# Attention and a two-layer feed-forward on one core: token and feature tiles padded by 32 and 64 bytes

## The chip, the cores and the metric

The kernel runs on one core of one Trainium2 chip. The metric is the time of one execution on the device in microseconds, lower is better; a measured time is the median of several executions.

## The reference, cut to what matters

Eight heads of attention over 8 sequences of 576 tokens with head size 64, then a feed-forward network over all 4608 tokens. Half of the heads see a local window of 32 positions, the other half every 32nd position.

```python
scores = scale * np.matmul(q, k.transpose(0, 1, 3, 2))
...
scores = np.where(masks[None, :, :, :], scores, -1000000000.0)
attn = exp(scores - max) / (sum + 1e-09)
attn_out = np.matmul(attn, v)
x = attn_out.transpose(0, 2, 1, 3).reshape(B * S, H * D)   # 4608 tokens x 512
h = np.maximum(x @ w_in, 0.0)                              # 512 -> 2048
return (h * h @ w_out).astype(np.float32)                  # 2048 -> 512
```

## The kernel before

The 4608 tokens are cut into 12 chunks of 384 (`TC`). For each chunk there are 16 groups of 128 hidden features. TensorE has two big jobs for each chunk and feature group.

`up` (through `products`, line 611) makes a tile of hidden features: 12 products of a 128x128 piece of `w_in` (the stationary operand, which is loaded into the array) with 384 tokens of x (the moving operand, which streams through it). Every number is held as a high and a low part, so x has four tiles for a chunk: `xlh`, `xll` from the local heads, `xsh`, `xsl` from the strided ones, each with two halves of 384 numbers for each of the 128 partitions. ScalarE then squares the rectified tile and writes its high part `gh`, VectorE its low part `gl`.

`down` (line 661) multiplies these: for each of three groups of 128 tokens, three products in which a 128x128 piece of `gh` or `gl` is stationary and 512 columns of `w_out` move.

From chunk 2 on the order is a cycle of four feature groups: four `up` (48 matmuls of line 611), four `down` (36 matmuls of line 661). Chunk 1 has the same in cycles of two. Ahead of each half of a cycle stands a visit of up to four small matmuls for the next chunks' attention: `s` (line 278, scores of a local head) and `o` (line 337, its output), as o, s, o, s. All other engines prepare x and the features beside this. Chunk 0 is written out by hand in the table `START`. The order on each engine is fixed by the program.

Where the tiles lie: pools are laid out one behind the other in each partition, first the weights (8192 bytes a tile), then `xpool` with two buffers of each of the four x tags, then `gpool` with three of `gh` and three of `gl`, then the rest. An x tile holds 2 x 384 numbers of four bytes, 3072 bytes, and a feature tile 384 numbers, 1536 bytes. All three sizes are multiples of 512, so each weight, x and feature tile starts at the same remainder modulo 512 bytes (it is 320 in the built program). The pieces taken from them also start at multiples of 512 bytes from the tile's start. So the moving and the stationary operand of every matmul of lines 611 and 661 are a multiple of 512 bytes apart. The distance is called zero in this text.

For the small matmuls it is not always so. The stationary `qx` piece of window w starts 384 w bytes into its tile and the moving `kx` piece 4 `at[w]` bytes into its own, and both tiles start at the same remainder. `windows` gives `at` = 0, 96, 192, 288 where both halves of a chunk lie behind each other in one sequence (chunks 6 to 11), and 0, 96, 224, 320 where they don't (chunks 0 to 5). So windows 2 and 3 of a local head have distance 0 in chunks 6 to 11 and distance 128 in chunks 2 to 5; they are visited between `up` and `down`.

```python
for n, (kt, w, s) in enumerate(parts):
    ...
    done = nc.tensor.matmul(h_ps[c, j][:, :TC], wi[p][w][:, wsl], x["ls"[kt // 2], s][:, kt % 2, :], ...)
...
    done = nc.tensor.matmul(into, g[:, t * P : (t + 1) * P], wo[p][w][:, wsl], ...)
```

Of the kernel before, what the change touches and what calls it, by code (L numbers as in the profile page):

```python
# [8 lines left out]
F32R = mybir.dt.float32r  # L9
# [13 lines left out]
P = 128  # L23
TC = 384
# [9 lines left out]
SCALE = 1.0 / 8.0  # L34
NEG = -8.0e9
JH = 8

NPLAIN = 2
NFIRST = 30
# [79 lines left out]
def attn_moe(ctx: ExitStack, tc, qk_l, v_l, qk_d, v_d, qk_p, v_p, f_s, q_s, k_s, v_s, w_in, w_out, masks, eye, out):  # L119
# [4 lines left out]
    xpool = pool("xpool", 2)  # L124
    gpool = pool("gpool", 3)
# [97 lines left out]
    def x_tiles(c):  # L223
        if c not in xt:
            xt[c] = {
                (kind, part): xpool.tile([P, 2, TC], F32R, name=f"x{kind}{part}{c}", tag=f"x{kind}{part}")
                for kind in "ls"
                for part in "hl"
            }
        return xt[c]  # L230
# [9 lines left out]
    class Head:  # L240
# [88 lines left out]
        def outputs(self, a, bank):  # L329
            par, hp = D * (self.h % 2), self.h // 2  # L330
            if a == 0 and not par:
                outs[self.c, hp] = self.buf(lpool, "st", TC, "st", bufs=1)
            o = psum(bank, f"o{a}{self.u}")

            def product(w):
                v, p = self.vx[:, w].rearrange("p t d -> p (t d)"), self.px[:, :, w * QC : (w + 1) * QC]
                return nc.tensor.matmul(o[:, 2 * QC * (w - a) : 2 * QC * (w - a + 1)], v, p, start=True, stop=True)  # L337

            def rest():
                x = x_tiles(self.c)  # L340
                st = outs[self.c, hp]
                ov = o[:, : 4 * QC].rearrange("p (w t q) -> p w t q", w=2, t=2)
                part = st[par : par + D, a * QC : (a + 2) * QC].rearrange("p (w q) -> p w q", w=2)
                nc.scalar.copy(part, ov[D:, :, 0, :])  # L344
                nc.vector.tensor_add(part, ov[:D, :, 1, :], part)
                nc.vector.tensor_add(part, ov[:D, :, 0, :], part)
                if par and a:
                    dst = [x["l", s][:, hp, :] for s in "hl"]
                    last["a"] = nc.scalar.copy(dst[0], st)
                    last["g"] = nc.gpsimd.tensor_sub(dst[1], st, f32(dst[0]))  # L350

            return [lambda w=w: product(w) for w in (a, a + 1)], rest
# [19 lines left out]
    class Pair:  # L372
# [80 lines left out]
        def out(self, a):  # L453
            x = x_tiles(self.at)
            if self.local:
                return self.s[a][:, :TC], [x["l", s][:, self.pr, :] for s in "hl"]
            r0 = D * self.pr
            by_i = lambda t: t[r0 : r0 + D].rearrange("p (s i r) -> p s i r", s=2, r=STR)
            return self.s[a][r0 : r0 + D, :TC].rearrange("p (s r i) -> p s i r", s=2, i=SI), [by_i(x["s", s][:, a, :]) for s in "hl"]
# [10 lines left out]
    class Range:  # L470


        def __init__(self, c, b, i0, i1, col):
            self.at, self.b, self.i0, self.i1, self.col = c, b, i0, i1, col
            self.ni, self.u = i1 - i0, f"{c}_{b}"
            self.short, self.prods = i1 == SI, {}
            self.scored = [(i, a, min(JH, i + 1 - a)) for i in range(i0, i1) for a in range(0, i + 1, JH)]
            self.mixed = []
            for i in range(i0, i1):
                step = -(-D // -(-(i + 1) // JH))  # L480
                self.mixed += [(i, a, min(step, D - a)) for a in range(0, D, step)]
# [24 lines left out]
        def m(self, n):  # L506
            i, a, m = self.scored[n]
            prod = spool.tile([P, JH * D], F32, name=f"pq{self.u}_{i}_{a}", tag="prod", bufs=2)
            pv = prod[:, : m * D].rearrange("p (j d) -> p j d", d=D)
# [28 lines left out]
        def p(self, n):  # L538
            i, a, nd = self.mixed[n]
            m, il = i + 1, i - self.i0  # L540
            prod = spool.tile([P, JH * D], F32, name=f"pp{self.u}_{i}_{a}", tag="prod", bufs=2)
            self.prods["p", n] = pv = prod[:, : m * nd].rearrange("p (d j) -> p d j", j=m)
# [11 lines left out]
        def out(self):  # L554
            x = x_tiles(self.at)
            cols = slice(self.col, self.col + self.ni * STR)
            return [x["s", s][:, :, cols] for s in "hl"], self.xf.rearrange("p a i r -> p a (i r)")
# [56 lines left out]
    def up(c, j):  # L614
        parts = [(kt, w, s) for kt in range(4) for w, s in ((0, "h"), (0, "l"), (1, "h"))]
        if j < 2:

            parts.sort(key=lambda i: i[0] < 2 and i[2] == "l")
        done = products(c, j, parts, True, True)
        g = h_ps.pop((c, j))[:, :TC]  # L620
        nc.scalar.activation(g, g, AF.Relu)  # L621
        nc.scalar.activation(g, g, AF.Square)  # L622
        feats[c, j] = feature_high(c, j, g), feature_low(c, j, g)
        return done

    def feature_high(c, j, g):
        gh = gpool.tile([P, TC], F32R, name=f"gh{c}_{j}", tag="gh")
        gl = gpool.tile([P, TC], F32R, name=f"gl{c}_{j}", tag="gl")
        g_tiles[c, j] = gh, gl
        return nc.scalar.copy(gh, g)  # L630

# [4 lines left out]
    def feature(j, what):  # L636

        g = h_ps[0, j][:, :TC]
        r = p_t[j % 2].rearrange("p w q -> p (w q)")
        if what == "R":  # L640
            nc.scalar.activation(r, g, AF.Relu)
        elif what == "G":
            nc.vector.scalar_tensor_tensor(out=g, in0=g, scalar=0.0, in1=r, op0=ALU.max, op1=ALU.mult)
        elif what == "K":
            last["a"] = feature_high(0, j, g)
        else:
            last["v"] = feature_low(0, j, g)
# [246 lines left out]
    for s in range(2 * NFT, NS, GROUP):  # L894
        c, j = divmod(s, NFT)
# [94 lines left out]
```

## Time and profile before

| what | value |
|---|---|
| median of 3 runs | 861.84 us (861.84 to 862.65) |
| span of the profiled execution, first to last instruction | 861.0 us |
| TensorE busy | 855.1 us of the span (99%) |
| VectorE, ScalarE, GpSimd busy | 643.0, 554.4, 662.8 us |
| granted TensorE clock | 1.00 over the span |

The profile gives the profiled execution's span; the median lies 0.84 us above it, which is taken as what lies around the first and the last instruction. Busy time of TensorE is the union of overlapping records, so it says that something was under way, not how fast. How fast is read from the starts of matmuls that follow each other.

### The profile page before, as it was taken

What the parts mean: (1) busy time and instruction counts of PE and PEld (TensorE: products, weight loads), DVE (VectorE), ACT (ScalarE), POOL (GpSimd) and SP (SyncE); (2) the same over time, 40 slices, a digit from 0 to 9 for tenths busy, and PEclk for the clock granted to TensorE, in tenths of its full rate; (3) what the DMA queues carried; (4) which work ended last, traced back from release to release, by engine and by line L of the source; (5) the groups of instructions that cost most, each with busy time, mean ns of one, the idle gap of its engine ahead of it and who ended that gap; (6) DMA issues with size and microseconds to landing.
All of it is one profiled execution on the core that took longest, in us unless ns stands there. A gap on an engine that the chain in (4) does not pass through costs nothing.

```text
span 861.0 us, 14577 instructions
## 1 busy us (share of the span) xinstructions
PE 855.1 (99%) x4748; PEld 781.5 (91%) x4748; DVE 643.0 (75%) x1893; ACT 554.4 (64%) x1473; POOL 662.8 (77%) x733
## 2 busy tenths in 40 slices
PE   9999999999999999999999999999999999999998
PEld 8988889999999999999999999999998999899987
DVE  7998788877787887797888788778878788852111
ACT  7997777676666765775577656665667567634423
POOL 5898788888788898898979989988987998850000
PEclk9999999999999999999999999999999999999999
DMA  9955522313122032113122111302211111000000
GB/s 356 364 218 158 171 81 83 108 37 108 56 88 81 27 133 76 32 63 113 31 69 71 58 54 56 99 27 81 78 54 63 45 60 38 1 2 37 1 1 37
DMA packets 27227, 71.32 MB, mean 83 GB/s; under 512 B 3024, under 2 KB 9680, under 8 KB 25616
## 3 DMA queue, kind: packets, MB, share of 16 engines
q1 hardware_dynamic: 26720, 70.00, 24.2%
q8 instruction: 37, 0.61, 0.3%
q10 hardware_dynamic: 432, 0.39, 0.1%
q14 instruction: 38, 0.31, 0.1%
HBM read 60.95 MB, written 9.44 MB: 82 GB/s over the span
## 4 chain that ended last, share of the span: by engine, by line
PE 95%; ACT 3%; DVE 1%; POOL 1%; issue 0%; POOLq 0%; ACTq 0%
PE h L611 45%; PE y L661 45%; PE s L278 2%; PE o L337 2%; ACT e L418 1%; ACT raw L184 1%; PE b L409 0%; PE w_ps L772 0%; ACT z L205 0%; POOL pq L510 0%; ACT pt L441 0%; DVE sc L515 0%; ACT xsh L463 0%; PE b L451 0%; DVE gl L634 0%
## 5 line engine op out<-in xcount | busy, mean ns | idle before, releaser
L661 PE MATMUL y<-w,gh 128*128 128x512 f32 x1152 | 364.8, 390 | 0.0
L661 PEld LDWEIGHTS y<-w,gh 128*128 128x128 f32 x1152 | 216.2, 188 | 43.8
L661 PE MATMUL y<-w,gl 128*128 128x512 f32 x576 | 224.3, 389 | 0.0
L611 PE MATMUL h<-xsh,w 128*128 128x384 f32 x768 | 223.2, 334 | 0.0
L611 PE MATMUL h<-xlh,w 128*128 128x384 f32 x768 | 216.9, 335 | 0.2 <-DVE gl L634 0.2
L510 POOL TENSOR_TENSOR pq<-ks,qs 128x512 f32<-128x512 f32 (+2 forms) x192 | 198.3, 1052 | 19.1 <-DVE sc L515 16.1
L543 POOL TENSOR_TENSOR pp<-vs,sc 128x448 f32<-128x448 f32 (+10 forms) x192 | 190.0, 1015 | 17.8 <-DVE qs L547 15.3
L634 DVE TENSOR_TENSOR gl<-h,gh 128x384 fp32r<-128x384 f32 x192 | 105.9, 552 | 79.2 <-ACT gh L630 76.9
L515 DVE TENSOR_REDUCE sc<-pq 128x8 f32<-128x512 f32 (+4 forms) x228 | 119.3, 534 | 33.9 <-POOL pq L510 30.6
L621 ACT ACTIVATE h<-h 128x384 f32<-128x384 f32 x176 | 83.8, 476 | 90.9 <-PE h L611 81.9
L611 PEld LDWEIGHTS h<-xlh,w 128*128 128x128 f32 x768 | 140.0, 188 | 1.8 <-DVE gl L634 0.6
L611 PEld LDWEIGHTS h<-xsh,w 128*128 128x128 f32 x768 | 141.2, 188 | 0.0
L661 PEld LDWEIGHTS y<-w,gl 128*128 128x128 f32 x576 | 108.2, 188 | 20.8
L611 PE MATMUL h<-xsl,w 128*128 128x384 f32 x384 | 125.7, 334 | 0.0
L611 PE MATMUL h<-xll,w 128*128 128x384 f32 x384 | 122.4, 335 | 0.0
L547 DVE TENSOR_REDUCE qs<-pp 128x64 f32<-128x448 f32 (+11 forms) x192 | 106.8, 563 | 20.4 <-POOL pp L543 17.9
L630 ACT CAST gh<-h 128x384 fp32r<-128x384 f32 x192 | 91.5, 478 | 14.0 <-PE y L661 7.5
L344 ACT COPY st<-o 64x192 f32<-64x192 f32 x80 | 25.1, 315 | 110.2 <-PE o L337 107.6
L311 DVE STREAM_TRANSPOSE p_t<-e 32x128 f32<-32x128 f32 x240 | 72.4, 301 | 21.9 <-ACT e L303 15.8
L622 ACT ACTIVATE h<-h 128x384 f32<-128x384 f32 x176 | 83.7, 475 | 4.7
L611 PEld LDWEIGHTS h<-xsl,w 128*128 128x128 f32 x384 | 71.9, 188 | 0.0
L611 PEld LDWEIGHTS h<-xll,w 128*128 128x128 f32 x384 | 71.6, 188 | 0.2
(111 smaller groups left out, 1122.2 us busy)
## 6 DMA issues: line engine op xcount, KB each, us to landing
qk<-qk_l SPq DMA_DIRECT2D x24, 400.0 KB, 3.1
y<-ysb SPq DMA_DIRECT2D x35, 256.0 KB, 2.1
raw<-w_in SPq DMA_DIRECT2D x7, 1024.0 KB, 10.3
qk<-qk_l SPq DMA_DIRECT2D x16, 416.0 KB, 3.3
vs<-v_s SPq DMA_DIRECT2D x10, 576.0 KB, 3.9
raw<-w_out SPq DMA_DIRECT2D x5, 1024.0 KB, 11.9
v<-v_l SPq DMA_DIRECT2D x40, 128.0 KB, 2.1
ks<-k_s SPq DMA_DIRECT2D x8, 576.0 KB, 3.8
```

Source lines behind the costliest of these rows:

```text
L311: nc.vector.transpose(out=pt[STR * k : STR * (k + 1), :, STR * r : STR * (r + 1)], in_=self.e.rearrange("p (w k) -> p w k", k=KW)[STR * r ...
L344: nc.scalar.copy(part, ov[D:, :, 0, :])
L510: nc.gpsimd.tensor_mul(pv, self.k[:, a : a + m, :], self.q[:, i - self.i0 : i - self.i0 + 1, :].broadcast_to([P, m, D]))
L515: nc.vector.tensor_reduce(out=self.sc[:, i - self.i0, a : a + m], in_=self.prods.pop(("m", n)), op=ALU.add, axis=AX.X)
L543: nc.gpsimd.tensor_mul(pv, self.v[:, a : a + nd, :m], self.sc[:, il : il + 1, :m].broadcast_to([P, nd, m]))
L547: nc.vector.tensor_reduce(out=self.q[:, i - self.i0, a : a + nd], in_=self.prods.pop(("p", n)), op=ALU.add, axis=AX.X)
L611: done = nc.tensor.matmul(h_ps[c, j][:, :TC], wi[p][w][:, wsl], x["ls"[kt // 2], s][:, kt % 2, :], start=fresh and n == 0, stop=full and n ...
L621: nc.scalar.activation(g, g, AF.Relu)
L622: nc.scalar.activation(g, g, AF.Square)
L630: return nc.scalar.copy(gh, g)
L634: return nc.vector.tensor_sub(gl, g, f32(gh))
L661: done = nc.tensor.matmul(into, g[:, t * P : (t + 1) * P], wo[p][w][:, wsl], start=j == fresh and k == 0, stop=j == NFT - 1 and k == 2)
```

## The change

Each x tile is allocated 8 numbers (32 bytes) longer and each feature tile 16 numbers (64 bytes) longer, and used without the added end. Nothing is read from or written to the added bytes. A tile takes 3104 and 1600 bytes in place of 3072 and 1536. The weights stay where they are (remainder 320). The eight x buffers now start at remainders 320, 352, 384, 416, 448, 480, 0 and 32, the six feature buffers at 64, 128, 192, 256, 320 and 384. So the moving operand of line 611 lies 0, 32, 64, 96, 128, 160, 192 or 224 bytes behind the stationary one modulo 512, and that of line 661 256, 192, 128, 64, 0 or 448 bytes: eight distances and six, with zero in both. Each pool behind `gpool` starts 640 bytes later, so the distances within and between those pools are as they were. The list of instructions, their order on each engine and the semaphores that they wait for are unchanged.

```diff
@@ -34,6 +34,7 @@
 JH = 8
+XGAP, GGAP = 8, 16
@@ -223,7 +224,7 @@
-                (kind, part): xpool.tile([P, 2, TC], F32R, name=f"x{kind}{part}{c}", tag=f"x{kind}{part}")
+                (kind, part): xpool.tile([P, 2 * TC + XGAP], F32R, name=f"x{kind}{part}{c}", tag=f"x{kind}{part}")[:, : 2 * TC].rearrange("p (t n) -> p t n", t=2)
@@ -624,8 +625,8 @@
     def feature_high(c, j, g):
-        gh = gpool.tile([P, TC], F32R, name=f"gh{c}_{j}", tag="gh")
-        gl = gpool.tile([P, TC], F32R, name=f"gl{c}_{j}", tag="gl")
+        gh = gpool.tile([P, TC + GGAP], F32R, name=f"gh{c}_{j}", tag="gh")[:, :TC]
+        gl = gpool.tile([P, TC + GGAP], F32R, name=f"gl{c}_{j}", tag="gl")[:, :TC]
```

## Rows read from the trace of the kernel before

**Rows 1.** The page: span, busy time by engine, granted clock in 40 slices.

```profile
span 861.0 us, 14577 instructions
PE 855.1 (99%) x4748; PEld 781.5 (91%) x4748; DVE 643.0 (75%) x1893; ACT 554.4 (64%) x1473; POOL 662.8 (77%) x733
...
PEclk9999999999999999999999999999999999999999
```

**Rows 2.** TensorE groups by shape: count, busy us, mean ns, idle us before them.

```profile
L661 PE MATMUL y<-w,gh 128*128 128x512 f32 x1148 | 364.0, 390 | 0.0
L661 PE MATMUL y<-w,gl 128*128 128x512 f32 x574 | 223.7, 390 | 0.0
L611 PE MATMUL h<-xsh,w 128*128 128x384 f32 x768 | 223.2, 334 | 0.0
L611 PE MATMUL h<-xlh,w 128*128 128x384 f32 x768 | 216.9, 335 | 0.2 <-DVE gl L634 0.2
L611 PE MATMUL h<-xsl,w 128*128 128x384 f32 x384 | 125.7, 334 | 0.0
L611 PE MATMUL h<-xll,w 128*128 128x384 f32 x384 | 122.4, 335 | 0.0
...
L772 PE MATMUL b<-p_t 128*128 128x128 bf16 x88 | 5.7, 219 | 0.0
```

**Rows 3.** Chain that ended last, in order of time: start us, us, what.

```profile
167.84 8.33 PE h L611 x48
...
176.60 8.18 PE y L661 x36
...
341.31 8.33 PE h L611 x48
...
350.06 8.20 PE y L661 x36
...
514.91 8.33 PE h L611 x48
...
791.29 8.34 PE h L611 x48
...
840.93 8.34 PE h L611 x48
```

**Rows 4.** Timeline of TensorE inside two stages: start us, us, instructions merged.

```profile
501.90 0.51 PE L611 MATMUL h<-xlh,w 128*128 128x384 f32 x2
...
503.98 0.51 PE L611 MATMUL h<-xlh,w 128*128 128x384 f32 x2
...
851.65 0.62 PE L661 MATMUL y<-w,gh 128*128 128x512 f32 x2
852.10 0.39 PE L661 MATMUL y<-w,gl 128*128 128x512 f32 x1
...
855.73 0.50 PE L661 MATMUL y<-w,gh 128*128 128x512 f32 x2
```

**Rows 5.** The same view where a stage begins without a visit.

```profile
791.13 0.87 PE L611 MATMUL h<-xlh,w 128*128 128x384 f32 x4
...
792.20 0.51 PE L611 MATMUL h<-xsh,w 128*128 128x384 f32 x2
...
799.48 0.39 PE L661 MATMUL y<-w,gh 128*128 128x512 f32 x1
...
801.78 0.39 PE L661 MATMUL y<-w,gl 128*128 128x512 f32 x1
```

**Rows 6.** The same view in chunk 0: bf16 products of zeros, one tile as both operands.

```profile
10.71 2.01 PE L772 MATMUL b<-p_t 128*128 128x128 bf16 x33
```

## The prediction

> **What bounds the kernel now.** I read the page first [rows 1]: TensorE is busy in 99% of the 861.0 us span and its clock is granted at 1.00 throughout, the upper of its two levels, 2.4 GHz. The next engine, GpSimd, has 77%. The groups of TensorE instructions [rows 2] show idle time ahead of the large matmuls of 0.2 us in all. So nothing outside TensorE sets the end; the time is the number of large matmuls times the distance between their starts. There are 768 + 768 + 384 + 384 = 2304 of line 611 and 1148 + 574 = 1722 full ones of line 661 [rows 2]. (Their mean of 334 and 390 ns is the life of one matmul, which overlaps the next, and not the distance.)
>
> The distance between starts comes from the timeline. Inside a stage of line 611, 12 matmuls lie between 501.90 and 503.98 us: 173.3 ns each. Inside a stage of line 661, 18 lie between 851.65 and 855.73 us: 226.7 ns each [rows 4]. The two shapes differ by 128 columns and 53.3 ns, so a column takes 0.417 ns, one period of 2.4 GHz, and 384 columns take 160.0 ns, 512 take 213.3. What is left is 13.3 ns for both shapes, though the one streams a third longer. 2304 x 173.3 + 1722 x 226.7 ns = 399.3 + 390.4 = 789.7 us of the span, of which 53.7 us (4026 x 13.33 ns) are this remainder. That is the only part that addresses could touch. The other 71 us are chunk 0's own work, the small matmuls and the end.
>
> **The change, part by part.** Nothing is added to or removed from any engine, no instruction is moved and no wait changes, so every term but one is zero by count. The one term is what the start address of x, gh and gl does to the instructions that touch them.
>
> *ScalarE, VectorE and GpSimd* write the padded tiles in the same shapes, at starts that are still multiples of 32 bytes. The trace has no row of the same write at another start, so I bound this by cover: even some ns more on each would lie beside TensorE, which idles 0.2 us in all for VectorE's `gl` [rows 2]. I take 0. Without that cover 192 feature tiles times a few ns would still be under 1 us.
>
> *TensorE, steady.* Three things speak for no change at all. First, the remainder is the same 13.3 ns for 384 and 512 columns; a collision of the two reads along the whole stream would have grown with it. Second, zero distance is not slow by itself: the products of zeros in chunk 0 use one tile as both operands, 33 of them take 2.01 us, and with 0.22 for the life of the last (mean 219 ns) [rows 2] that is 1.79 / 32 = 56 ns, only 2.7 ns over their 53.3 ns of columns [rows 6]. They are bf16, so this is a far row. Third, the starts look as if they fell on a grid of 13.33 ns. 160.0, 213.3, 173.3 and 226.7 are 12, 16, 13 and 17 of these. The cycles are too: 167.84 to 341.31 us holds 10 cycles of 17.347 us, 341.31 to 514.91 holds 10 of 17.360, and 791.29 to 840.93 holds 3 of 16.547 [rows 3]: 1301, 1302 and 1241 times 13.333 ns. Each settled matmul then waits for the next place in a grid, and a few ns more or less of reading vanish in that wait. Since the columns alone fill a whole number of places, no smaller settled step than one more place is left. This is inferred from starts alone; what makes the grid the trace doesn't say. I take 0 for the steady step.
>
> *TensorE, at the borders of stages.* Here the steps are not settled: the first 6 of a stage of line 611 take 1.07 us, 178 ns each, and the first 10 of line 661 2.30 us, 230 ns each [rows 5], before they fall to 173.3 and 226.7. Another distance may lengthen or shorten this run by a place of the grid. The kernel has 40 cycles of 48 + 36 matmuls and 8 half-length ones in chunk 1, so one place in each cycle is 48 x 13.33 = 0.64 us; I allow two either way, 1.3 us, and take 0.
>
> That addresses can matter here is in the trace. The cycles up to 341 us are 13 ns shorter than the later ones [rows 3], and the same instructions stand in both; what differs on TensorE is that two of the k windows start 128 bytes later, so that the two `s` matmuls between `up` and `down` have a distance of 128 where later ones have zero. The stage of line 661 behind them takes 8.18 us in place of 8.20 [rows 3]. So distance 128 was *cheaper* there by 13 ns for two matmuls, one place of the grid in a cycle of 17 us.
>
> The Trainium skill, page "SBUF — State Buffer", section "Who interferes with whom", says that TensorE has two independent read ports, one for the moving operand and one for weight loads, and never waits on another engine. By it the whole change is worth zero and the sum stays 861.8. The 13 ns a cycle are not quite in agreement with that, though the remaining rows are.
>
> **Sum.** 861.0 us of span + 0 (other engines) + 0 (steady) + 0 ± 1.3 (borders) = 861.0, and 0.84 us around the span as in the profile before: 861.8, the median of the runs shown. A kernel whose runs lie between 861.84 and 862.65 tells 0.2%, 1.7 us, from no change.
>
> **Rivals.**
>
> *A, slower: the new distances keep the steps unsettled.* The settled step may depend on both operands being in the same place modulo 512 at each matmul; within a stage of line 611 four x tiles would now alternate between four distances, and in line 661 `gh` and `gl` between two. If the pattern never settles, steps are those at the start of a stage: 178 for 173.3 and 230 for 226.7 [rows 4, 5]. Seven of eight x buffers and five of six feature buffers leave zero: 2304 x 7/8 = 2016 matmuls x 5 ns = 10.1 us and 1722 x 5/6 = 1435 x 3.7 = 5.3 us, together 15.4 us, so 877.2 us. If about half of the distances do it, 869.5. It decides from the point where a conflict delays a matmul by more than the slack in its place of the grid: between 0 and 13.3 - 2.7 = 10.6 ns, by the zero products. For it: the steps at the start of a stage show that another state exists and costs 4 to 5 ns, and that it lasts 6 to 10 matmuls, so it is not quickly lost. Against: it dies out although x tiles alternate in address, and it also occurs at distance zero, so distance isn't what makes it.
>
> *B, faster: zero is the costly distance.* The 13 ns a cycle for two `s` matmuls are 6.5 ns each; at 3451 matmuls that leave zero this is 22.4 us, 839.4 us; with a third of it, 854. If the whole excess over the bf16 row went, 10.6 x 3451 = 36.6 us, 825. For it: that row is the only pair in this trace in which the same work stands at two distances, and it favours the other one. Against: 256 and 192 columns leave little time to hide a weight load, 384 and 512 leave much; a gain in a wait of that kind would not carry over. And the gain may be only one place of the grid, set off by 1 ns.
>
> The Trainium skill, page "TensorE: Matmul & The Clock Gate", section "Back-to-back issue gap", gives the isolated warm gap as N / 2.4 + 2.5 ns, 162.5 for 384 columns and 215.8 for 512. The bf16 row agrees (56 ns), the steady rows of lines 611 and 661 don't, by 10.8 ns. Were that excess the price of distance zero, rival B in full is what the page's figure would give, by estimate 861.8 - 3451 x 0.0108 = 824.6.
>
> *C, the change doesn't do what it says.* If the allocator rounded the tiles up, distances would stay. The built program has the new remainders, so I give this no chance of its own; its time would be that of the forecast.
>
> **How the numbers follow.** Forecast, steady step kept: 0.59, with 860.5 to 863.1 as its own range (± 1.3). Rival A: 0.24, over 870 in about 0.10, since half of the distances at fault gives 869.5. Rival B: 0.17, under 853 in about 0.10, since a third of its row's price gives 854. The predicted time is the forecast's, 861.8. The range goes from 853 to 870 and leaves out 0.2. The forecast's own range lies within 1.7 us of no change, so the chances are faster 0.17, same 0.59, slower 0.24.
>
> **What would show it.** Right: 12 starts of line 611 still cover 2.08 us and 18 of line 661 4.08 us in chunks with even and with odd numbers (they use the two buffers of each x tag), cycles of 17.360 us or a multiple of 13.3 ns beside it. Rival A: starts in the middle of a stage that lie 177 to 180 or 230 apart and stages of 8.33 and 8.20 us that grow to 8.5, in some chunks or feature buffers and not in others. Rival B: the same stages shorter than 8.33 and 8.20. If the groups of TensorE gain idle time ahead of them, with ScalarE or VectorE as releaser, the cover was thinner than I read, and the prediction is wrong for a reason outside TensorE. It is also wrong if the granted clock is no longer 1.00.

## The result and the profile after

The changed kernel takes 872.83 us in the median of 4 runs (872.58 to 873.18); the kernel before, run beside it, takes 862.25 (861.84 to 863.63). The ratio on record is 1.0117, with an interval of 1.0103 to 1.0131, and the two medians are 10.6 us apart: slower by 1.2%. The forecast was no change. Rival A, steps that don't settle, is what came.

The page of the changed kernel, its first lines (they answer to [rows 1]):

```profile
span 870.7 us, 14577 instructions
PE 865.3 (99%) x4748; PEld 786.2 (90%) x4748; DVE 645.5 (74%) x1893; ACT 554.8 (64%) x1473; POOL 663.5 (76%) x733
...
PEclk9999999999999999999999999999999999999999
```

The number of instructions and the granted clock are as before, and TensorE is as busy. The groups of TensorE instructions by shape (they answer to [rows 2]: count, busy us, mean ns, idle us before them) show that nothing makes it wait either:

```profile
L662 PE MATMUL y<-w,gh 128*128 128x512 f32 x1148 | 368.2, 394 | 0.0
L612 PE MATMUL h<-xsh,w 128*128 128x384 f32 x768 | 226.1, 339 | 0.0
...
L612 PE MATMUL h<-xlh,w 128*128 128x384 f32 x768 | 219.4, 339 | 0.2 <-DVE gl L635 0.2
```

So the matmuls themselves follow each other more slowly. (All lines behind the new constant have moved by one: 611 is 612, 661 is 662.) The chain that ended last, start us, us, what (it answers to [rows 3]):

```profile
660.83 8.44 PE h L612 x48
...
678.41 8.50 PE h L612 x48
...
687.33 8.34 PE y L662 x36
...
696.08 8.38 PE h L612 x48
...
704.87 8.33 PE y L662 x36
```

Stages that took 8.33 and 8.18 to 8.20 us take 8.38 to 8.50 and about 8.32. 38 pieces of 48 that the chain shows whole add up to 316.66 us before and 320.92 after, 39 pieces of 36 to 318.96 and 324.40. Together that is 9.7 us more, all that the span grew by (861.0 to 870.7). Inside the stages (timeline of TensorE, where [rows 4] had 173.3 and 226.7 ns):

```profile
610.01 0.34 PE L612 MATMUL h<-xlh,w 128*128 128x384 f32 x1
...
612.12 0.34 PE L612 MATMUL h<-xlh,w 128*128 128x384 f32 x1
...
670.67 0.62 PE L662 MATMUL y<-w,gh 128*128 128x512 f32 x2
...
673.44 0.39 PE L662 MATMUL y<-w,gh 128*128 128x512 f32 x1
...
680.37 0.34 PE L612 MATMUL h<-xlh,w 128*128 128x384 f32 x1
...
682.50 0.34 PE L612 MATMUL h<-xlh,w 128*128 128x384 f32 x1
```

Twelve matmuls lie in each of the three stretches: 2.11 us, 176 ns each, in an even chunk, 2.13 us, 177 ns each, in an odd one, and 2.77 us, 231 ns each, of line 662. These are deep in their stages, where the step was settled before.

### The profile page after: what moved, and what is told of

Same layout as the page of the kernel before. It is cut to its first block, busy times and chain, and to the rows that moved or that the text cites. A ratio compares the mean times of both kernels' runs of the same rounds, so it can differ in the third digit from the quotient of the medians.

```text
span 870.7 us, 14577 instructions
## 1 busy us (share of the span) xinstructions
PE 865.3 (99%) x4748; PEld 786.2 (90%) x4748; DVE 645.5 (74%) x1893; ACT 554.8 (64%) x1473; POOL 663.5 (76%) x733
## 4 chain that ended last, share of the span: by engine, by line
PE 96%; ACT 1%; DVE 1%; POOL 1%; issue 0%; POOLq 0%; ACTq 0%; DVEq 0%
PE h L612 45%; PE y L662 45%; PE s L279 2%; PE o L338 2%; ACT e L419 1%; PE b L439 0%; PE w_ps L773 0%; PE b L452 0%; PE b L410 0%; POOL pq L511 0%; ACT raw L185 0%; POOL vx L320 0%; POOL kx L267 0%; DVE gl L635 0%; ACT z L206 0%
## 5 line engine op out<-in xcount | busy, mean ns | idle before, releaser
L662 PE MATMUL y<-w,gh 128*128 128x512 f32 x1152 | 368.9, 394 | 0.0
L662 PEld LDWEIGHTS y<-w,gh 128*128 128x128 f32 x1152 | 216.5, 188 | 47.0 <-POOL sc L505 0.3
L662 PE MATMUL y<-w,gl 128*128 128x512 f32 x576 | 226.2, 393 | 0.0
L612 PE MATMUL h<-xsh,w 128*128 128x384 f32 x768 | 226.1, 339 | 0.0
L612 PE MATMUL h<-xlh,w 128*128 128x384 f32 x768 | 219.4, 339 | 0.2 <-DVE gl L635 0.2
L612 PEld LDWEIGHTS h<-xlh,w 128*128 128x128 f32 x768 | 140.8, 188 | 1.9 <-DVE gl L635 0.5
L612 PEld LDWEIGHTS h<-xsh,w 128*128 128x128 f32 x768 | 141.6, 188 | 0.0
L662 PEld LDWEIGHTS y<-w,gl 128*128 128x128 f32 x576 | 108.3, 188 | 22.6
L612 PE MATMUL h<-xsl,w 128*128 128x384 f32 x384 | 127.1, 338 | 0.0
L612 PE MATMUL h<-xll,w 128*128 128x384 f32 x384 | 123.6, 338 | 0.0
L612 PEld LDWEIGHTS h<-xsl,w 128*128 128x128 f32 x384 | 72.0, 188 | 0.0
L612 PEld LDWEIGHTS h<-xll,w 128*128 128x128 f32 x384 | 71.8, 188 | 0.3
```

## The experiments

Two theories stood at first. Theory D: each distance other than zero keeps the steps from settling. Theory V: one distance of any size settles, and it is the change of distance from one matmul to the next that costs. The settled steps below are worked out from the starts of the matmuls in the second half of each stage of 48 (line 611 of the kernel before) or 36 (line 661), as the median over the 20 to 41 stages of a run. In the views of the runs these lines stand some lines further down (L612 to L624, L662 to L665).

**The two gaps apart (e1, e2) and one distance for all (e3, e4).**

```diff
-XGAP, GGAP = 8, 16
+XGAP, GGAP = 8, 0        # e1; e2 has 0, 16
```

> The change's gap for x alone: x tiles at eight distances, 0 to 224 bytes; all feature tiles at one distance, 256. Theory D (each distance other than zero keeps steps unsettled): stages of line 612 at 8.38 to 8.50 us as in the changed kernel and stages of line 662 near 8.32 too, 870 us or more. Theory V (steps stay unsettled where the distance varies from one matmul to the next, one distance of any size settles): stages of line 612 as in the changed kernel, stages of line 662 back at 8.20; about 862.3 + 5.1 = 867 us, by the excess of 5.1 us over the settled step that the changed kernel's line 612 shows beyond the kernel before.

> The change's gap for gh and gl alone: x tiles at distance zero, six feature tiles at distances 0, 64, 128, 192, 256 and 320 below. Theory D and theory V alike: stages of line 612 at 8.33 us, stages of line 662 at about 8.32; about 862.3 + 5.6 = 868 us. If the two gaps hurt one another only together, both this run and the run with x alone stay under 864.

```diff
+    gap = pool("gap", 1).tile([P, 16], F32, name="gap")   # e3; e4 has 32
     xpool = pool("xpool", 2)
```

> No gaps, but 64 unused bytes ahead of all x tiles: every x and feature tile at one distance, 64 bytes, from the weights. Theory D: both kinds of stage unsettled, 868 to 880 us. Theory V: settled steps of 173.3 and 226.7 ns, 861 to 863 us. Theory B (zero is a costly distance): under 858.

> The same with 128 unused bytes: one distance of 128 bytes for all. Theory D: 868 to 880 us. Theory V: 861 to 863 us. Theory B, from the two score matmuls that were cheaper at distance 128: under 858.

| run | us | ratio to before (interval) | step of 384 columns | step of 512 columns |
|---|---|---|---|---|
| e1, x alone | 867.17 | 1.0051 (1.0036 to 1.0066) | 177.1 in odd, 176.0 in even chunks | 226.6 |
| e2, features alone | 868.72 | 1.0070 (1.0055 to 1.0085) | 173.3 | 231.3 |
| e3, all shifted by 64 | 871.30 | 1.0102 (1.0085 to 1.0119) | 173.3 | 233.2 |
| e4, all shifted by 128 | 875.48 | 1.0149 (1.0134 to 1.0164) | 176.1 | 233.5 |

The kernel before ran at 862.65 beside them. The gaps act each on the stage whose operand they move, and add up: 4.5 + 6.1 = 10.6 us, what the whole change cost. Theory V falls as it stood: e4 has one distance for every matmul of both lines and is the slowest of the four. Theory D in its plain form falls too: e3 settles at 173.3 ns with x at 64, and the features of e1, which by the eight gaps ahead of them all lie at 256, settle at 226.6. The chain of e3 (64 bytes) and then of e4 (128 bytes):

```profile
658.97 8.32 PE h L612 x48
667.71 8.39 PE y L662 x36
676.52 8.32 PE h L612 x48
```

```profile
663.32 8.45 PE h L612 x48
672.18 8.38 PE y L662 x36
680.98 8.44 PE h L612 x48
```

In e3 only the stages of 36 are long (8.39 for 8.20), in e4 both kinds. A distance here is the start of the moving operand minus that of the stationary one, modulo 512. In e3 x moves and lies 64 bytes behind its weights, distance 64; in line 661 `w_out` moves and lies 64 bytes ahead of the features, distance 448. So either the sign of the distance counts (theory S) or the shape (theory K).

**A map of distances (e5 to e8).** The x pool is split in two, one for odd and one for even chunks, with unused bytes ahead of each and, but for e6, ahead of the features. The edit of e5; e6 to e8 differ in the sizes:

```diff
+    pool("pad0", 1).tile([P, 8], F32, name="pad0")
-    xpool = pool("xpool", 2)
+    xpool = pool("xpool", 1)
+    pool("pad1", 1).tile([P, 16], F32, name="pad1")
+    xpool0 = pool("xpool0", 1)
+    pool("pad2", 1).tile([P, 32], F32, name="pad2")
     gpool = pool("gpool", 3)
...
-  xpool.tile([P, 2, TC]
+  (xpool if c % 2 else xpool0).tile([P, 2, TC]
```

> One distance for each chunk: x of odd chunks 32 bytes, x of even chunks 96, all features 288 (32 modulo 256). Nothing else changed. Theory S (the signed distance decides, modulo 256: 0 and 64 settle at 173.3 and 226.7 ns, the rest don't): 176 to 178 ns in both kinds of chunk, 230 to 234 in line 662. Theory K (the shape decides: 384 columns settle at short distances of either sign, 512 columns only at 0 modulo 256): odd chunks settle at 173.3, even ones need not, line 662 at 230 to 234.

> The same with x of odd chunks at 160, of even chunks at 192 (64 short of 256), features at 320 (64 modulo 256). Theory S: even chunks unsettled, 175 ns or more, and line 662 settles at 226.7. Theory K: even chunks settle at 173.3 and line 662 stays at 233. This run tells the two apart.

> The same with x of odd chunks at 224, of even chunks at 448, features at 352 (96 modulo 256). If the pattern repeats every 256 bytes, even chunks here do as even chunks at 192 did in the run before. Theory S: both unsettled, 175 ns or more, line 662 230 to 234. Theory K: even chunks at 173.3, line 662 230 to 234.

> The same with x of odd chunks at 256, of even chunks at 320, features at 160. If the pattern repeats every 256 bytes, odd chunks settle at 173.3 (as distance 0) and even chunks at 173.3 (as distance 64); if it repeats only every 512 bytes, one of them needn't. Line 662 230 to 234 by both theories.

One execution each: 877.04, 867.00, 873.12 and 872.82 us beside 862.70 of the kernel before. By distance, with those of the other runs (a number by itself is the median of the stages):

| distance modulo 512 | 384 columns, ns | 512 columns, ns |
|---|---|---|
| 0 | 173.3 | 226.6 |
| 32 (512 columns: 288) | 173.3 in 10 stages, 176.5 to 176.8 in 10 | 233.4 |
| 64 (512 columns: 320) | 173.3 | 228.9 |
| 96 (512 columns: 352) | 176.7 | 233.1 |
| 128 (512 columns: 384) | 176.1 | 233.5 |
| 160 | 173.3 in 19 stages, 176.6 in one | 234.3 |
| 192 (512 columns: 448) | 176.7 in 15, 174.6 in 3, 173.3 in 2 | 233.2 |
| 224 | 173.3 | 233.4 |
| 256 | 173.3 | 226.6 |
| 320 | 173.3 | |
| 448 | 174.7 in 19 stages, 176.7 in one | |

Theory K as it stood falls, since e6 brings 512 columns from 233 to 228.9 at the other sign, and most stages of its even chunks, at 192, stay at 176.7. Theory S is half right: 0 and 256 are alike and 64 is better than 192 for both shapes, but 384 columns also settle at 160 and 224, and 512 columns at 64 come close to the settled step without reaching it. So it is a table by distance and shape and not a rule by sign. The repeat after 256 bytes holds for 0 and 64. At 192 and 448 most stages differ (176.7 and 174.7), but each of the two steps is seen at both.

The map does not add up to the change. In e1 odd chunks run at 177.1 ns, slower than any one distance in the map (176.8 at most), although the eight distances of x hold some that settle alone. Over all stages x has 176.2 ns there, where the mean of the map's rows from 0 to 224 is by estimate about 174.6, and the features of e2 have 231.2, where the mean of their six distances in the map is by estimate 230.3. So a distance that changes from one matmul to the next seems to cost something of its own, which is the other half of theory V; no run takes that apart.

The row at 32 has the same distance, the same instructions and two outcomes. The chain of e5, the four stages of line 611 of odd chunk 9:

```profile
664.15 8.47 PE h L615 x48
...
681.86 8.32 PE h L615 x48
...
699.43 8.32 PE h L615 x48
...
716.98 8.47 PE h L615 x48
```

Four stages of one chunk, 8.47, 8.32, 8.32 and 8.47 us. The step isn't fixed by the distance alone: a run of matmuls falls into one of several repeating patterns. From the starts in the trace, the slow stages go 175, 177, 175, 180, 174, 178 and over again; the second stage has 173 or 174 at each step, the third 172, 172, 175, 172, 175, 171, with the same mean of 173.3. How a stage is entered seems to have a part in which. Chunks 5, 7 and 9 have the same order of slow and settled stages; chunk 3, where two of the `s` matmuls in the visits have distance 128, settles in all four, and chunk 11, without visits, in none (176.8). The stages at 160, 192 and 448 that leave their row's usual step also lie where the visits differ, up to the second stage of chunk 4 or from the third of chunk 10 on. No run changes the visits alone, so this is not shown.

**Control: distance or address (e9).**

```diff
+    pool("pad0", 1).tile([P, 32], F32, name="pad0")
     wpool = pool("wpool", 1)
```

> 128 unused bytes ahead of the weights as well: weights, x and features all start 128 bytes later, so the distance stays zero while every address is that of the 128-byte run for x and features. If the distance between the two operands decides: 862 to 863 us, settled steps of 173.3 and 226.7 ns. If the address of x and of the features itself decides: about 875 us, as there.

862.84 us, ratio 1.0004 (0.9995 to 1.0013), steps 173.3 and 226.6. Every x and feature tile stands at the address that it has in e4, where the kernel takes 875.48; only the weights came along. The chain of e9:

```profile
672.32 8.33 PE h L612 x48
681.06 8.20 PE y L662 x36
689.67 8.33 PE h L612 x48
```

So, for 128 bytes, it is the distance between the two operands of TensorE, and neither an address nor the writes of ScalarE, VectorE and GpSimd to the moved tiles. For the other distances this is taken over from that run.

**Versions by the map (e10, e12).**

```diff
+    pool("pad0", 1).tile([P, 56], F32, name="pad0")
     xpool = pool("xpool", 2)
+    pool("pad1", 1).tile([P, 8], F32, name="pad1")         # e12 has 16
     gpool = pool("gpool", 3)
```

> All x at the distance 224, at which line 611's stages ran at 8.32 us without a slower beginning, all features at 256, where line 661 settles. Theory D, with these distances read off the map runs: 48-matmul stages at 8.32 in place of 8.35 us, 36-matmul stages at 8.19; 48 stages by 0.03 us, about 861 to 862 us, at best 0.2% under the kernel before. If the saving at the stages' beginnings comes back elsewhere: 862 to 863.

> All x at 224 and the features at 224 modulo 256 too, the one distance that line 661 has not been run at. Theory S (same rule for both shapes): line 662 settles at 226.7 ns and its stages begin without slower steps, 8.16 to 8.19 us; 860 to 862 us. If 512 columns behave differently from 384: 231 to 234 ns, 8.3 to 8.4 us a stage, 868 to 871 us.

e10: 861.26 us beside 862.60, ratio 0.9981 (0.9972 to 0.9990), 0.2% under the kernel before by an interval that leaves out 1, as far as it was expected to be (the 8.35 us of the expectation are 8.33 in the chain of the kernel before, [rows 3]). e12: 871.13, ratio 1.0096 (1.0082 to 1.0109); at 224 the 512 columns run at 233.4, so 224 is good for line 611 and bad for line 661. Theory S falls here in its general form. The chain of e10:

```profile
669.86 8.32 PE h L613 x48
678.59 8.19 PE y L663 x36
687.19 8.32 PE h L613 x48
```

**Which stationary operand (e11, e13 to e15).** While a matmul streams, the next one's stationary operand is loaded. In the kernel before, a matmul of `xsh` starts at 500.52 us; beside it starts the load for the next one, of `xsl`, which takes 0.19 us, and that matmul starts at 500.69 (timeline, PE the matmuls, PEld the weight loads):

```profile
500.52 0.33 PE L611 MATMUL h<-xsh,w 128*128 128x384 f32 x1
500.52 0.19 PEld L611 LDWEIGHTS h<-xsl,w 128*128 128x128 f32 x1
...
500.69 0.33 PE L611 MATMUL h<-xsl,w 128*128 128x384 f32 x1
```

These runs give a matmul different distances to its own and to the next one's; zero and 128 are meant modulo 256 bytes here. e11 moves the low x tiles and the low parts of the first four `w_in` pieces by 128 bytes; e13 and e14 let local and strided x take turns in groups 2 to 7 and move one of them with half of each of those pieces:

```diff
+        if 2 <= j < 8:
+            parts = [i for two in zip(parts[:6], parts[6:]) for i in two]
...
-  t = wpool.tile([P, 2, 1024], F32R, name=f"w{which}_{p}", tag=f"w{k}")
+  side = [pl.tile([P, 2, WP], F32R, ...) for pl, nm in ((wpool, "w"), (sidepool, "v"))]
...
-  xpool.tile([P, 2, TC]
+  (xpool if kind == "l" else xqpool).tile([P, 2, TC]      # e14: kind == "s"
```

> Low x tiles and the low parts of the first four pieces of w_in lie 128 bytes off the rest. In feature groups 2 to 7 of a chunk the moving operand then has distance zero to the stationary operand that is loaded while it streams (the next matmul's), but 128 to its own in two of three matmuls; in groups 8 to 15 one matmul in three has 128 to both. If what counts is the load that runs beside the stream: groups 4 to 7 settle at 173.3 ns, groups 8 to 15 stay at 175 or more. If the matmul's own stationary operand counts: groups 4 to 7 stay at 175 or more too. Features at distance zero, line 661 settles at 226.7. Time 862 to 868 us.

> In feature groups 2 to 7 of a chunk local and strided x take turns, strided x and its half of w_in lie 128 bytes off the rest (only the first four pieces of w_in): each matmul has distance zero to its own stationary operand and 128 to the next one's, which is loaded while it streams. If the own distance decides: groups 4 to 7 settle at 173.3 ns. If the next one's decides: 175 to 177 ns, as at 128 for all. Groups 8 to 15 have 0 to both for local x and 128 to both for strided x: over 174. Time 862 to 870 us.

> The same with local x off by 128 in place of strided x: in groups 2 to 7 each matmul has distance 128 to its own stationary operand and zero to the next one's. If the own distance decides: groups 4 to 7 at 175 to 177 ns. If the next one's decides: they settle at 173.3. Time 862 to 870 us.

> Control: the kernel before with local and strided x taking turns in groups 2 to 7, all distances zero. Both theories: settled at 173.3 ns in all groups, 862 to 863 us.

| run | distance to own, to next, groups 4 to 7 | step, groups 4 to 7 | groups 8 to 15 | us, one execution |
|---|---|---|---|---|
| e15 | 0, 0 | 173.3 | 173.3 | 862.23 |
| e13 | 0, 128 | 175.4 | 174.7 | 866.07 |
| e14 | 128, 0 | 176.7 | 175.1 | 866.91 |
| e11 | 128 in two of three, 0 | 175.4 | 175.8 | 865.14 |

The chain at groups 4 to 7 of chunk 9, of e15, then e13, then e14:

```profile
670.49 8.33 PE h L611 x48
```

```profile
673.49 8.42 PE h L624 x48
```

```profile
674.26 8.48 PE h L624 x48
```

The kernel before ran at 862.60 beside e11 and 862.91 beside the other three. The new order alone changes nothing (e15). Neither theory holds by itself: zero to the own operand doesn't settle the step when the next is at 128, and the reverse doesn't either. Both distances have a part, or what counts is something that changes with both, such as the step from one matmul's reads to the next one's; which, these runs leave open.

## Why the prediction was wrong, point by point

*What bounds the kernel* held. TensorE has 0.2 us of idle time ahead of the large matmuls in both traces, and the growth of the span is in its stages.

*Other engines: 0* held. The writes of `gh` take 478 ns in both traces and those of `gl` 552 and 553, and TensorE gains no idle time for them; e9, with their tiles moved by 128 bytes, is at 1.0004.

*TensorE, steady: 0* is the step that failed. The steps in the second halves of the stages of chunks 2 to 11, taken for whole stages, make 11.16 us more than before (4.83 in line 611, 6.33 in line 661). With what the beginnings give back (next point), the change costs 10.6 us, 4.5 for x (e1) and 6.1 for the features (e2). I gave three reasons. That the remainder is 13.3 ns for both shapes is true of settled steps at distance zero and says nothing of others: at 128 the remainder is 16.1 ns for 384 columns and 20.2 for 512. The zero products, with one tile as both operands, showed that zero isn't slow; I needed that the other distances are not slow, and had no row for it. The grid was the weightiest and is wrong as I used it: I read the multiples of 13.33 ns as places in which some nanoseconds of delay vanish. They are what the steps come to when a stage settles, at 0 and 256 bytes and at some others; elsewhere the steps stay off these multiples for a whole stage (228.9, 231.3, 176.1 as means) and the delays are paid.

*Borders of stages: 0 ± 1.3* was off too, to the other side. What the stages of chunks 2 to 11 take beyond the step of their second halves was 1.66 us before and is -0.13 after: 1.8 us less. A stage that doesn't settle has no slower beginning; its beginning's steps go on. The time between the stages is the same, 45.16 and 45.14 us. In e10, with the same settled steps as before, the slower beginnings shrink by 0.7 us and the pauses between stages by 0.35.

*Rival A* had the mechanism and the place, and its sign came as written: stages of up to 8.50 us, steps of about 175 to 177 and 231 in their middle. Its price was 10.1 us for x and 5.3 for the features; they measured 4.5 and 6.1, so x was priced at over twice what it cost. It took the steps of a stage's beginning, 178 and 230, for every matmul that leaves zero; the mean over x was 176.2, and some of its distances settle when they stand alone. The 5 and 3.7 ns that it used are 4.7 and 3.3 by its own rows (178 less 173.3, 230 less 226.7), which would be 14.2 us in place of 15.4. What I set against it, that unsettled steps also occur at distance zero and die out there, was the wrong inference: whether they die out depends on the distance.

*Rival B* fails: no distance gave a settled step under 173.3 or 226.6 ns. The 13 ns a cycle by which the early cycles are shorter [rows 3] are a matter of how the following stage begins: the stage of line 661 is 21 ns shorter from its first to its last start (7.947 for 7.968 us), and the pause ahead of it 8 ns longer. They are no price of a matmul at distance 128; that the two `s` matmuls at 128 bring them about was not tested.

*The Trainium skill*, page "SBUF — State Buffer", section "Who interferes with whom", has TensorE's two read ports independent and says that nobody makes it wait. It idles 0.2 us in all ahead of the large matmuls here, so that part agrees. That the two reads don't disturb each other, as I read the independence, does not agree: e4 and e9 have x and features at the same addresses and differ in the distance to the weights, and in the ratio to the kernel before, 1.0149 and 1.0004. The Trainium skill, page "TensorE: Matmul & The Clock Gate", section "Back-to-back issue gap", gives an isolated gap by which the step would be, by estimate, 162.5 and 215.8 ns. No distance tried comes under 173.3 and 226.6, so none of them closes that gap.

*Around the span* I took 0.84 us, the span of one execution from the median of others. Each run's own time and span are 1.9 to 2.0 us apart (872.66 and 870.7). It cancels in the comparison.

## What to carry to other kernels

Where TensorE is saturated with one weight load for each matmul, look at the distance between the starts of moving and stationary operands modulo 256 bytes before a tile's size is changed: a tile that grows by some bytes moves all that lie behind it. The map is that of this kernel, 128x128 stationary pieces with 384 and 512 columns; for other shapes it has to be measured. Sizes that are multiples of 512 keep all distances at zero, which was good for both shapes here; of the other distances tried only 256 was good for both. Read the step from the starts of a run of matmuls deep in a stage, since busy shares and waits don't show it.

## What was not expected of the hardware

- The distance between the two operands of a matmul, with the instructions unchanged, is worth 1.5% in e4 (875.48 for 862.65 us; 2.8 ns a matmul of 384 columns and 6.9 of 512), and 1.7% in the one execution of e5 (877.04 for 862.70).
- At one distance (32 bytes) stages of the same instructions ran at 173.3 or at 176.5 to 176.8 ns a matmul, and at 192 at 173.3, 174.6 or 176.7.
- The settled remainder over 0.417 ns a column is 13.3 ns at every distance that settles, for both shapes; what it is made of stays open.
